# Mamba2 scan and cosine router: two buffers per scan input instead of three, with B's transpose loaded last and two vector steps moved

## The chip, the cores and the metric

The kernel runs on one NeuronCore of a Trainium2 chip. The core has a matrix engine (TensorE, PE in the profile, with its weight loads as PEld), a vector engine (VectorE, DVE), a scalar engine (ScalarE, ACT), a general engine (GpSimd, POOL) and a sequencer that mostly issues DMAs (SyncE, SP). The metric is the device time of one launch in microseconds; lower is better.

## The reference, cut to what matters

The first part is a chunked state-space scan over x (4 batches, 8 heads, 768 steps, 32 wide) with decays `a` and 16-wide matrices B and C. In a chunk, with `cum` the cumulative sum of log(a) and L[i,j] = exp(cum_i − cum_j) for i ≥ j:

```
y_intra = ((C_i · B_j) * L[i,j]) x_j          # inside the chunk
y_inter = exp(cum_i) * (C_i state)            # from the state before the chunk
state   = exp(sum la) * state + sum_j exp(cum_last - cum_j) B_j x_j
```

The second part takes y as 3072 rows of 256. Each row goes to one of 8 experts, by the largest cosine with that expert's embedding, and gets gate * (relu(row w1[e]) w2[e]), where w1 is 256 x 1024, w2 is 1024 x 256 and the gate is the softmax weight of the chosen expert. All data are float32.

## The kernel before, in words

**Scan.** The sequence is cut into six chunks of Q = 128 steps (`NC` = 6), and all batches and heads of a chunk are done together. `load(k, c)` brings in a chunk's five inputs: `ct` (C transposed), `bi` (B transposed), `x`, `xa` (the upper half of x's columns for the chunk's first 64 steps, put on the other half of the partitions) and `b` (B by step). They come from the pool `inp` of three buffers per name, all on SP's queue and in program order. A load into a buffer waits until the readers of the chunk that held it are done. The readers are: `scale_c` on DVE for `ct`; `split_b` on ACT and `inner` on PE for `bi`; `scale_x` and `scale_first_half` on POOL for `x`; `scale_first_half` for `xa`; `sums` on PE for `b`.

`decays` makes cumulative products on DVE for chunks 0 to 3, and later for 4 and 5. `spread_decays` (PE) copies them to all partitions, and `scale_c` multiplies C by them. `inner` (PE) makes the products of C and B into the PSUM tile `pg`, for two batches at a time, and `mask_inner` (DVE, line 341) multiplies them by the causal mask into `g`. `outputs` and `first_outputs` (PE, lines 369 and 382) multiply `g` by the scaled x into `py`; `first_outputs` reads `xb`, a tile of which one half per partition group must be zero. `clear_first_half` zeroes it once for each of its two buffers, and POOL then fills the other half per chunk (line 258). The state lives in `V`: `sums` (PE) makes a chunk's contribution in the PSUM tiles `pz`, `add_sums` (DVE, line 316) adds it to the decayed state `U`, and `decay_states` makes `T` (DVE) and `U` (POOL, line 293) for the next chunk. `finish` (PE, line 400) turns a chunk's outputs to rows and takes their products with the embeddings, half of it in `py` and half in the `pz` banks; `keep_rows` (ACT) and `send_rows` (SP, line 415) bring the rows to memory. `pick`, `count_picks`, `rank_rows`, `places` and `locate` work out each row's expert and its place there.

**Order.** Every engine's instructions run in the order in which the Python program writes them: a manual schedule is in force, and the framework adds waits only. `mamba` is that order. In it, loop step c does chunk c and prepares chunk c + 1; `load(k, c + 2)` stands at the head of the step, and `add_sums(k, c)` stands before the step's first `mask_inner` for c of 3 and 4, and behind `scale_c` of the next chunk for c of 1 and 2. `warm_up` puts matmuls of a constant on PE that nothing reads.

**Experts.** Rows of an expert are gathered by indirect DMA (line 844), turned, multiplied by w1 (line 951) and w2 (lines 968 and 1013; in four of the experts the second product is done in seven block products), turned back and scattered (line 1056). The weights of the first experts are loaded on SP's queue during the scan: w1 of expert 0 at step 3, w2 of expert 0 at step 4.

Of the kernel before, what the change touches and what calls it, by code (L numbers as in the profile page):

```python
# [19 lines left out]
NC = S // Q  # L20
# [19 lines left out]
def load_decays(k):  # L40
    nc = k.nc
    k.a0 = k.mc.tile([128, 2, Q], F32, name="a0")
    a = k.a.rearrange("b h (c s) -> c (b h) s", c=NC)
    nc.gpsimd.memset(k.a0[:, 1, :], 1.0)
    for c in range(NC):
        (nc.sync if c % 2 == 0 else nc.scalar).dma_start(k.a0[c % 4 : 128 : 4, c // 4, :], a[c])


def load(k, c):
    nc = k.nc  # L50
    t = k.ld[c]

    def in_(name, shape):
        return k.inp.tile([128] + shape, F32, name=name, tag=name)

    t.ct, t.bi, t.b = in_("ct", [NB, Q]), in_("bi", [NB, Q]), in_("b", [NB, 128])
    t.x, t.xa = in_("x", [NB, DM]), in_("xa", [NB, 128])
    for dst, src in ((t.ct, k.CT), (t.bi, k.BT), (t.x, k.x)):
        nc.sync.dma_start(dst[:].rearrange("p b m -> p (b m)"), src[c])
    nc.sync.dma_start(t.xa[HQ:, :, :], k.x[c, 0:HQ, :].rearrange("p (b m) -> p b m", b=NB)[:, :, 128:])  # L60
    nc.sync.dma_start(t.b[:].rearrange("p b m -> p (b m)"), k.B[c])


def load_weights(k, e, parts=(0, 1)):
# [60 lines left out]
def clear_first_half(k, i):  # L125
    k.nc.vector.memset(k.xb[i][0:HQ, :, :, 1, :], 0.0)
    k.nc.vector.memset(k.xb[i][HQ:, :, :, 0, :], 0.0)


def warm_up(k, n):  # L130
    for _ in range(n):
        k.nc.tensor.matmul(k.pz[1][:], lhsT=k.warm[:, 0:Q], rhs=k.warm[:], start=True, stop=True)
# [96 lines left out]
def mask_c(k, c):  # L229
    t = k.ld[c]  # L230
    for v in range(2):
        k.nc.scalar.activation(t.cp[:, :, 3 + v, :], t.cp[:, :, 1, :], ACT.Copy, scale=k.tmask[:, v : v + 1])
# [395 lines left out]
def mamba(k):  # L628
    nc = k.nc
    k.f = k.mc.tile([128, 2, FX], F32, name="f")  # L630
    k.rT = k.mc.tile([128, 2, 2, 128], F32, name="rT")
    k.V = k.mc.tile([128, NB, 2 * D], F32, name="V")
    k.ends = k.mc.tile([128, NC, NB, 3], F32, name="ends")
    k.rr, k.wm, k.ends_in = {}, {}, {}
    for c in range(NC):
        k.ld[c] = Net()
        k.ld[c].g = []
    load_decays(k)
    expert_emb(k)
    load(k, 0)  # L640
    build_consts(k)
    warm_up(k, 13)
    decays(k, 0)
    load(k, 1)
    square_emb(k)
    route_consts(k)
    spread_decays(k, 0)
    warm_up(k, 3)
    split_b(k, 0)
    scale_c(k, 0)  # L650
    mask_c(k, 0)
    inverses(k, 0)
    block_ends(k, 0)
    scale_emb(k)
    clear_first_half(k, 0)
    spread_decays(k, 1)
    warm_up(k, 1)
    inner(k, 0, 0)
    mask_inner(k, 0, 0)
    turn_inverses(k, 0, k.py[:, 0, 0:256])  # L660
    scale_x(k, 0, nc.gpsimd)
    scale_first_half(k, 0, nc.gpsimd)
    scale_c(k, 1)
    spread_ends(k, 0, k.pz[0][:, 0:48])
    turn_emb(k, k.pz[1][:, 400:416])
    warm_up(k, 2)

    for c in range(NC):
        t = k.ld[c]
        n = c + 1  # L670
        if c + 2 < NC:
            load(k, c + 2)
        if c in (3, 4):
            load_weights(k, 0, (c - 3,))
        if c == 5:
            load_weights(k, 1, (0,))
        if 2 <= c < NC - 1:
            spread_decays(k, n)
        if 3 <= c < NC - 1:
            add_sums(k, c)  # L680
        if c >= 2:
            inner(k, c, 0)
        if c == NC - 1:
            early_places(k, c - 3)
        if c >= 2:
            mask_inner(k, c, 0)
        if 3 <= c < NC - 1:
            locate(k, c - 3)
            keep_located(k, c - 3)
        if n < NC:  # L690
            scale_x(k, n, nc.gpsimd)
        if 1 <= c < NC - 1:
            scale_c(k, n)
        if c in (1, 2):
            add_sums(k, c)
        if c >= 2:
            pick(k, c - 2)
        if c > 0:
            finish(k, c - 1)
            keep_rows(k, c - 1)  # L700
            send_rows(k, c - 1)
        if c == 2:
            spread_ends(k, 1, k.pz[0][:, 400:424])
        inner(k, c, 1)
        mask_inner(k, c, 1)
        if c == 0:
            sums(k, 0)
        if n < NC:
            split_b(k, n)
            mask_c(k, n)  # L710
        if c == NC - 1:
            k.early_x = early_rows(k)
            gather_halves(k, k.early_x, k.gi0, 0, 0, 3 * NB * Q)
        if c >= 2:
            count_picks(k, c - 2)
        if c == NC - 1:
            gather_halves(k, k.early_x, k.gi0, 0, 1, 3 * NB * Q)
        if n < NC:
            scale_first_half(k, n, nc.gpsimd)
            if c in (0, 3):  # L720
                between(k, n, 4 if c == 0 else NC)
            pass_c(k, n)
        if 3 <= c < NC - 1:
            add_located(k, c - 3)
        if c > 0:
            from_states(k, c)
        if 2 <= c < NC - 1:
            rank_rows(k, c - 2)
            keep_ranks(k, c - 2)
        outputs(k, c, 0)  # L730
        if c == 0:
            clear_first_half(k, 1)
            spread_decays(k, 2)
            inner(k, 1, 0)
            mask_inner(k, 1, 0)
            add_sums(k, 0)
        outputs(k, c, 1)
        if c == NC - 1:
            early = early_jobs(k)
            early[0].turn_x()  # L740
            rank_rows(k, c - 2)
            keep_ranks(k, c - 2)
        first_outputs(k, c)
        keep_outputs(k, c)
        if c + 2 < NC:
            sums(k, n)
        if c == 2:
            turn_inverses(k, 1, k.pz[0][:, 0:256])
        if c == NC - 1:
            pick(k, c - 1)  # L750
            count_picks(k, c - 1)
        if c >= 2:
            places(k, c - 2)
        if c == 4:
            shift_places(k)
        if c == 1:
            decays(k, 1)
            block_ends(k, 1)
            inverses(k, 1)
        if n < NC:  # L760
            decay_states(k, n)
    return early
# [583 lines left out]
@with_exitstack  # L1346
def kernel(
    ctx: ExitStack,
    tc: tile.TileContext,
    x: bass.AP,  # L1350
    a: bass.AP,
    B: bass.AP,
    BT: bass.AP,
    CT: bass.AP,
    moe_expert_emb: bass.AP,
    moe_tau: bass.AP,
    moe_w1: bass.AP,
    moe_w2: bass.AP,
    out: bass.AP,
):  # L1360
    k = Net()
    k.tc, k.nc = tc, tc.nc
    k.x, k.a, k.B, k.BT, k.CT = x, a, B, BT, CT
    k.emb, k.tau, k.w1, k.w2, k.out = moe_expert_emb, moe_tau, moe_w1, moe_w2, out
    k.ld, k.w1t, k.w2t = {}, {}, {}

    k.y_d = tc.dram_tile([T, W], F32, name="y_rows")
    k.of_row = tc.dram_tile([E * T, 1], I32, name="of_row")
    k.const = ctx.enter_context(tc.tile_pool(name="const", bufs=1))
    k.wp = ctx.enter_context(tc.tile_pool(name="wp", bufs=3))  # L1370
    k.ep = ctx.enter_context(tc.tile_pool(name="ep", bufs=1))
    with ExitStack() as m:
        k.mc = m.enter_context(tc.tile_pool(name="mc", bufs=1))
        k.inp = m.enter_context(tc.tile_pool(name="inp", bufs=3))
        k.work = m.enter_context(tc.tile_pool(name="work", bufs=2))
        ps = m.enter_context(tc.tile_pool(name="ps", bufs=1, space=PSUM))
        k.py = ps.tile([128, 2, 512], F32, name="py")
        k.pz = [ps.tile([128, 512], F32, name=f"pz{i}") for i in range(2)]
        k.pgs = m.enter_context(ExitStack())
        k.pg = k.pgs.enter_context(tc.tile_pool(name="pg", bufs=1, space=PSUM)).tile([128, 4, 512], F32, name="pg")  # L1380
        k.late_psum = m.enter_context(ExitStack())
        with tc.manual_schedule():
            early = mamba(k)
            late = scan_end(k, early)
    with (
        tc.tile_pool(name="moe", bufs=2, reuse_waits="tile") as p,
        tc.tile_pool(name="moe_ps", bufs=1, space=PSUM, reuse_waits="tile") as ps,
    ):
        k.p, k.ps = p, ps
        with tc.manual_schedule():  # L1390
            last = moe(k, early[1], late)
        leftover(k)
        with tc.manual_schedule():
            moe_end(k, last)
# [43 lines left out]
```

## Time and profile before

| what | value |
|---|---|
| median of 3 runs | 279.59 us (275.69 to 284.28) |
| the profiled execution's own time | 278.24 us |
| its span, first to last instruction | 276.5 us |
| PE busy | 256.2 us (93%) |
| DVE busy | 148.9 us (54%) |
| POOL busy | 159.0 us (58%) |
| ACT busy | 70.9 us (26%) |
| mean granted PE clock | 0.977 |
| moved by DMA | 35.87 MB, 29.05 MB of it read from HBM |

The scan takes roughly the first 80 us; the rest is the experts. Busy shares are means over both, and a matmul's end in the trace is modelled, so a high PE share does not mean that PE is at its limit. In a row of the timeline the first number is the start and the second the duration, in us; what stands in brackets is the idle time of the engine ahead of it and the engine, tile and line whose end released it. "issue" there means that the trace shows no wait.

### The profile page before, as it was taken

Reading aid. Unit: us, or ns where it says so; the run is one execution under the profiler, and the core shown is the slowest. Engines: PE = TensorE matmul, PEld = TensorE weight load, DVE = VectorE, ACT = ScalarE, POOL = GpSimd, SP = SyncE. Lnnn points to the kernel's source line nnn. Section 1 sums busy time; section 2 is a strip of 40 time slices with the busy share of each in tenths; the row PEclk is TensorE's granted clock in tenths of the full one; section 3 lists DMA queues with packets and bytes.
Section 4 is the critical chain, followed back from the end, with each engine's and each line's share of the span. In section 5 each row is a group of like instructions: output and inputs, shape, how many; then the busy total and the mean of one; then the engine's idle time right before and its main releaser. Section 6 shows DMA issues by size and latency. Waiting matters only on the chain.

```text
span 276.5 us, 6216 instructions
## 1 busy us (share of the span) xinstructions
PE 256.2 (93%) x2446; PEld 209.6 (76%) x2446; DVE 148.9 (54%) x396; ACT 70.9 (26%) x216; POOL 159.0 (58%) x193
## 2 busy tenths in 40 slices
PE   6759989898699999999999999999999999999990
PEld 2548778788599999999469659757957965975890
DVE  5873867888464402144656458468448645833011
ACT  3604344343055132340231131031023123101100
POOL 8998254764503542848828858866956966005022
PEclk9997999999779999999999999999999999999998
DMA  4992849936309920698718518615640201002011
GB/s 120 322 359 59 278 133 274 281 110 163 109 10 282 267 74 9 146 263 189 203 27 183 171 54 177 193 47 124 141 148 26 63 3 53 1 0 56 8 33 31
DMA packets 22304, 35.87 MB, mean 130 GB/s; under 512 B 2548, under 2 KB 15551, under 8 KB 22273
## 3 DMA queue, kind: packets, MB, share of 16 engines
q1 hardware_dynamic: 19024, 28.73, 37.5%
q0 software_dynamic: 3072, 6.67, 9.5%
q8 instruction: 20, 0.33, 0.6%
q14 instruction: 12, 0.09, 0.1%
q10 hardware_dynamic: 176, 0.06, 0.1%
HBM read 29.05 MB, written 6.65 MB: 129 GB/s over the span
## 4 chain that ended last, share of the span: by engine, by line
PE 56%; issue 15%; DVE 10%; POOL 10%; DMA 6%; ACT 1%; POOLq 1%; DVEq 0%
PE hp L951 22%; PE yp L1013 12%; PE eb L951 5%; DMA out_dram<-yo,to 4%; PE eb L968 4%; DVE g L341 3%; POOL xb L258 2%; PE yp L968 2%; DMA xg<-y_rows,gi 2%; POOL xg L844 2%; POOL out_dram L1056 2%; PE py L382 2%; PE pg L331 2%; POOL spread L91 1%; PE ot L1053 1%
## 5 line engine op out<-in xcount | busy, mean ns | idle before, releaser
L951 PE MATMUL hp<-xT,w 128*128 128x416 f32 (+1 forms) x256 | 83.9, 469 | 0.0
L1056 POOL DMA_INDIRECT out_dram<-yo,to x32 | 34.5, 1080 | 55.3 <-DVE yo L1055 54.1
L951 PEld LDWEIGHTS hp<-xT,w 128*128 128x128 f32 x256 | 45.8, 191 | 21.6 <-issue 21.6
L844 POOL DMA_INDIRECT xg<-y_rows,gi x32 | 43.8, 1370 | 15.6 <-issue 7.3
L955 ACT ACTIVATE hT<-hp 128x416 f32<-128x416 f32 (+1 forms) x32 | 15.2, 474 | 81.8 <-PE hp L951 81.7
L957 DVE TENSOR_SCALAR hT<-hp 128x416 f32<-128x416 f32 (+1 forms) x32 | 17.2, 537 | 29.6 <-PE hp L951 29.6
L341 DVE TENSOR_TENSOR g<-pg,mask 128x1536 f32<-128x1536 f32 x12 | 21.1, 1756 | 9.5 <-PE pg L331 9.5
L968 PE MATMUL yp<-hT,w 128*128 128x208 f32 x128 | 23.4, 340 | 0.3 <-PEq L1270 0.3
L968 PEld LDWEIGHTS yp<-hT,w 128*128 128x128 f32 x128 | 22.3, 190 | 0.9 <-issue 0.9
L1013 PE MATMUL yp<-T,S 128*128 128x208 f32 x120 | 22.7, 339 | 0.0
L1013 PEld LDWEIGHTS yp<-T,S 128*128 128x128 f32 x120 | 21.2, 190 | 0.0
L1083 POOL TENSOR_TENSOR gr<-gr,half 104x4 f32<-104x4 f32 x8 | 8.7, 1090 | 14.2 <-ACT sq L1077 14.1
L1013 PE MATMUL yp<-hT,w 128*128 128x208 f32 x80 | 16.1, 344 | 0.2 <-ACT p L1029 0.2
L1013 PEld LDWEIGHTS yp<-hT,w 128*128 128x128 f32 x80 | 13.7, 190 | 1.0 <-ACT p L1029 0.9
L951 PE MATMUL eb<-xT,w 128*128 128x208 f32 x64 | 14.3, 374 | 0.0
L523 POOL TENSOR_TENSOR pre<-pre,ob 128x8 bf16<-128x8 bf16 x24 | 4.8, 199 | 16.3 <-DVE ob L518 14.8
L1077 ACT ACTIVATE sq<-xg 104x256 f32<-104x256 f32 x32 | 13.0, 407 | 0.0
L988 POOL TENSOR_TENSOR S<-w 128x512 f32<-128x512 f32 x10 | 12.7, 1269 | 0.1
L951 PEld LDWEIGHTS eb<-xT,w 128*128 128x128 f32 x64 | 12.0, 207 | 0.2
L968 PE MATMUL eb<-hT,w 128*128 128x208 f32 x64 | 12.0, 341 | 0.0
L246 POOL TENSOR_TENSOR xs<-x,rT 128x1024 f32<-128x1024 f32 x6 | 11.8, 1966 | 0.1
L393 ACT COPY yT<-py 128x512 f32<-128x512 f32 x12 | 6.4, 589 | 20.1 <-PE py L382 20.1
(224 smaller groups left out, 429.3 us busy)
## 6 DMA issues: line engine op xcount, KB each, us to landing
w<-in_moe_w_dram SPq DMA_DIRECT2D x16, 512.0 KB, 6.9
w<-in_moe_w_dram SPq DMA_DIRECT2D x8, 1024.0 KB, 7.6
y_rows<-rows SPq DMA_DIRECT2D x6, 528.0 KB, 4.2
x<-in_x_dram SPq DMA_DIRECT2D x6, 512.0 KB, 6.0
ct<-in_CT_dram SPq DMA_DIRECT2D x6, 256.0 KB, 5.2
bi<-in_BT_dram SPq DMA_DIRECT2D x6, 256.0 KB, 5.1
b<-in_B_dram SPq DMA_DIRECT2D x6, 256.0 KB, 6.2
xa<-in_x_dram SPq DMA_DIRECT2D x6, 128.0 KB, 7.4
```

Of the source, the lines that this page charges most:

```text
L246: engine.tensor_tensor(out=t.xs[:].rearrange("p b (h d) -> p b h d", h=NH), in0=t.x[:].rearrange("p b (h d) -> p b h d", h=NH), in1=r_of(k ...
L341: k.nc.vector.tensor_tensor(out=g[:], in0=k.pg[:, :, 0:384].rearrange("p q (u m) -> p q u m", u=2), in1=k.mask[:].unsqueeze(1).unsqueeze(1 ...
L844: k.nc.gpsimd.indirect_dma_start(out=x, out_offset=None, in_=k.y_d[0:rows, :], in_offset=bass.IndirectOffsetOnAxis(ap=at, axis=0), bounds_ ...
L951: nc.tensor.matmul(t, lhsT=s.w1[:, j, 128 * f : 128 * f + 128], rhs=s.xT[:, j, :], start=(j == 0), stop=(j == KD - 1))
L955: nc.scalar.activation(s.hT[:, f, :], t, ACT.Relu)
L957: nc.vector.tensor_scalar_max(s.hT[:, f, :], t, 0.0)
L968: nc.tensor.matmul(t, lhsT=s.w2[:, f, 128 * j : 128 * j + 128], rhs=s.hT[:, f, r], start=(f == 0), stop=(f == KF - 1))
L988: k.nc.gpsimd.tensor_tensor(out=s.S[:, n], in0=x, in1=y, op=op)
L1013: nc.tensor.matmul(t, lhsT=a[:, f], rhs=b[:, f], start=start and f == 0, stop=(f == 3), skip_group_check=True)
L1056: d = nc.gpsimd.indirect_dma_start(out=k.out[:, :], out_offset=bass.IndirectOffsetOnAxis(ap=s.to[:, i : i + 1], axis=0), in_=y[:], in_offs ...
L1077: s.k.nc.scalar.activation(sq[:], s.x[:, i, :].rearrange("p (j w) -> p j w", j=KD)[:, :, 0:128], ACT.Square, accum_out=s.r[:, i : i + 1],)
L1083: s.k.nc.gpsimd.tensor_tensor(out=s.r[:], in0=s.r[:], in1=s.k.half[0 : s.tr, 0 : s.nt], op=ALU.pow)
```

## The change

Five edits in the scan:

1. The pool `inp` has two buffers per name instead of three.
2. In `load`, `bi` is second for chunks 0 and 1, as before, and last for chunks 2 to 5.
3. `clear_first_half(k, 0)` moves on DVE from behind `scale_emb` to ahead of `decays(k, 0)`.
4. `add_sums(k, 2)` moves on DVE ahead of step 2's first `mask_inner`.
5. The first run of warm-up matmuls is one shorter (12), the last one longer (3).

The order of every other instruction on every engine is the same, the experts included.

```diff
-    for dst, src in ((t.ct, k.CT), (t.bi, k.BT), (t.x, k.x)):
+    def whole(dst, src):
         nc.sync.dma_start(dst[:].rearrange("p b m -> p (b m)"), src[c])
+
+    whole(t.ct, k.CT)
+    if c < 2:
+        whole(t.bi, k.BT)
+    whole(t.x, k.x)
     nc.sync.dma_start(t.xa[HQ:, :, :], k.x[c, 0:HQ, :].rearrange("p (b m) -> p b m", b=NB)[:, :, 128:])
-    nc.sync.dma_start(t.b[:].rearrange("p b m -> p (b m)"), k.B[c])
+    whole(t.b, k.B)
+    if c >= 2:
+        whole(t.bi, k.BT)
...
-    warm_up(k, 13)
+    warm_up(k, 12)
+    clear_first_half(k, 0)
     decays(k, 0)
...
     scale_emb(k)
-    clear_first_half(k, 0)
     spread_decays(k, 1)
...
-    warm_up(k, 2)
+    warm_up(k, 3)
...
-        if 3 <= c < NC - 1:
+        if 2 <= c < NC - 1:
             add_sums(k, c)
...
-        if c in (1, 2):
+        if c == 1:
             add_sums(k, c)
...
-        k.inp = m.enter_context(tc.tile_pool(name="inp", bufs=3))
+        k.inp = m.enter_context(tc.tile_pool(name="inp", bufs=2))
```

## The prediction

> **What bounds the kernel now.** I read the page's slices first, then PE's waits, then the timeline around the longest wait, then the DMA view of that stretch. Of the page, PE's busy share, its granted clock and the DMA share, over 40 slices of 6.9 us:
>
> ```profile
> PE   6759989898699999999999999999999999999990
> PEclk9997999999779999999999999999999999999998
> DMA  4992849936309920698718518615640201002011
> ```
>
> From slice 11 on (76 us) PE is full, so what the edits save before that point comes off the end, unless it is lost on the way. The scan is not full. PE's waits, with total, count and longest in us:
>
> ```profile
> PE py L369 <- issue: 2.5, 1, 2.5
> ...
> PE pz L400 <- DVE V L316: 1.6, 1, 1.6
> ```
>
> The timelines of PE, POOL and DVE show where these two sit and what runs beside them:
>
> ```profile
> 17.57 0.31 PE L369 MATMUL py<-g,xs 128*32 128x64 f32 x6
> 20.38 0.63 PE L369 MATMUL py<-g,xs 128*32 128x64 f32 x26 [2.50 <-issue]
> 20.95 1.44 PE L382 MATMUL py<-g,xb 128*64 128x64 f32 x32
> ...
> 35.70 0.50 PE L400 MATMUL pz<-turn,yT 128*128 128x136 f32 x2 [1.55 <-DVE V L316]
> ```
> ```profile
> 21.93 0.62 POOL L293 TENSOR_TENSOR U<-T,ends 128x256 f32<-128x256 f32 x1 [0.36 <-DVE T L287]
> ```
> ```profile
> 27.56 1.76 DVE L341 TENSOR_TENSOR g<-pg,mask 128x1536 f32<-128x1536 f32 x1 [3.80 <-PE pg L331]
> ...
> 38.68 1.76 DVE L341 TENSOR_TENSOR g<-pg,mask 128x1536 f32<-128x1536 f32 x1 [1.85 <-PE pg L331]
> ```
>
> PE stops in the middle of one group (6 of its 32 matmuls done) with all inputs there. The DMA view of 17.7 to 18.9 us:
>
> ```profile
> q1 hardware_dynamic: 239, 0.43, 99.8%
> q8 instruction: 1, 0.02, 5.5%
> ```
>
> One 16 KB packet of instructions moves just then, through engines that q1 (the input loads) fills. From 13.6 to 17.7 us q1 takes 106.2% and no instruction packet appears. The last row ahead of the stop is the 449th of PE's rows, its semaphore instructions counted; PE's next stop on "issue" (51.41 to 52.04 us) comes exactly 1,536 rows later, 6 x 256. So these are stops for code, at multiples of one block. The block of the first stop would have been asked for at its predecessor's entry, 256 rows earlier, at 13.6 us, while the loads of four chunks (5.6 MB, issued from 2.96 to 16.96 us) kept the DMA at 324 to 343 GB/s until 21 us.
>
> **The change part by part.**
>
> *Two buffers.* Chunks 2 and 3 no longer load at once. SP holds `x` of chunk 2 until POOL has read chunk 0's: `scale_first_half`'s first row ends at 14.60 us (before, SP issued that load at 10.23). Then follow `xa` behind 15.75, `b` (sums of chunk 0 on PE, 14.94) and `bi`, till about 17.4; `ct` of chunk 3 at about 17.5, its `x` behind 18.81. So at 13.6 us two chunks and one `ct` are in flight, 3.0 MB since 3 us, nearly drained at 0.33 MB/us. The code packet then takes about 1 us to start, 1.05 to move and, as at the stall (18.84 to 20.38), 1.5 to be usable: 17.2 us, where PE needs it at 17.7.
>
> [...]
>
> What is late next is POOL. It works without a gap from 7.67 to 21.0 us, which puts `U` of chunk 1 at 21.93 to 22.55 whatever PE does. `V` follows at 22.6 to 23.1 (0.48 us, as chunk 2's). PE without the stop does `outputs` until 18.3, `first_outputs` (1.15 us where the clock is full, at 29.96) until 19.4; ACT's `yT` takes 1.07, the `py` half of `finish` 1.19, until 21.7. Its `pz` half waits for `V`, 23.1 to 24.3, against 26.39 before. So `inner` and the `g` row at 27.56 come 2.1 us sooner. A rest of the stop up to 1.4 us would be hidden (21.7 to 23.1). Nothing can make it more than 2.1. From below I take 1.3, for the clock, as follows.
>
> The window 18.21 to 21.63 held 1.25 us of PE, and in the next one the granted clock is 0.50. [...] Other windows: 1.81 of 3.41 fell, 2.23 held. After the change the window 21.63 to 25.04 holds about 2.0, between these. [...] I take full speed and keep 0.8 for the range.
>
> *B turned last.* `bi(c+2)` waits for `split_b` and step c's second `inner`. Queued behind it on SP are `send_rows(c-1)`, the next chunk's loads and the weights of expert 0. The order is worth something only against `bi` second, where `x` would wait behind it. Slack of each load (landing takes 4.8 to 8.2 us for `x`): `x(2)` issued 14.7, needed 22.51; `x(3)` 18.9 against 31; `x(4)` 26 against 41; `x(5)` 37 against 52; `bi(4)` 35.4 against 44.4. Rows are read by the first gather at 66 us. Cost 0; had `x(2)` landed 3 us late, POOL's idle 5.14 us before chunk 2's `U` takes it.
>
> The weights are the exception. w1 of expert 0 (42.20 us) and w2 (48.19) stood 6 us apart. Now w1 waits behind `bi(5)`, about 45, so `bi`, w1, rows and w2 make one burst of 2.8 MB, 8 us. PE enters a block near 48.8 (52.04 less 3.3); as at the first stop, 4.15 us to start, 1.05 to move, 1.5 to be usable, 55.5 us, needed at 55.1. I charge 0.3; ends: -0.4 (today's 0.41 us stop goes, if it counted) and 2.5.
>
> *States of chunk 2 ahead of the mask.* Now: mask 33.09 to 34.85, `scale_c`, then `V` at 35.36, so `pz` in `finish` waits 1.55 and `inner` starts at 37.44. After: `V` follows `U` at once, then mask (0.5 later), `scale_c` and `pick` (1.08), which ends when it did. PE runs `pz` without waiting, and `inner` is no longer late: `g` at 38.68 comes 1.2 sooner. Chunk 3, already in this order, agrees: `V` 44.12 to second mask 48.49 is 4.37 us; here it would be 33.17 to 37.5. Range 0.8 to 1.3. From then on DVE carries each step (10.7 us from `T` at 42.98 to 53.67), and the shift goes through to the gather.
>
> *Clearing and warm-ups.* The two memsets take 9.63 to 10.74, 1.11 us, and go into DVE's 1.19 us wait for `a` ahead of 3.94: free, at most 0.1. The first mask can start at 9.9 instead of 10.78. One more warm-up (0.29) then ends near 12.45, when `scale_c` is done, so second `inner` comes 0.7 sooner. POOL's gapless row swallows it: 0, at best 0.7. The shorter first run still spans its warm-up (eight slow, four fast matmuls).
>
> Sum: 2.1 + 1.2 + 0 - 0.3 = 3.0 us. The profiled execution took 278.24, so 275.2 on its terms. With it the four times of this kernel are 275.69, 278.24, 279.59, 284.28, middle 278.9: 275.9.
>
> **Rivals.**
>
> *The typical run gains more (30%).* The four times spread by 8.6 us. Waiting for code hangs on what else the DMA does, and a low clock follows each stop; if that makes the spread, a kernel with little of it lands near its fastest: 275.69 - 3.0 = 272.7. For: code and clock are the only waits here that chance moves. Against: the clock also falls at 72.83 to 79.65, behind the gather, which the change leaves.
>
> *No difference (15%).* The stop is not the loads' doing, or the clock falls in its place: 1.2 - 0.3 remains, 278.0. Against: packets at 26.82 and 38.40, with the DMA freer, came with no stop.
>
> *Slower (10%).* Loads that follow their readers come in bursts at the step's end, where PE changes blocks. A full stop costs 2.5 plus some 1.7 for a window of 3.4 us at half clock. Two on the path: 8.4 - 3.3 = 5.1 slower, 284.0. It decides where fetching takes longer than PE needs for a block, 3.6 us at the shortest (38.10 to 41.71). Against: bursts are issued just behind a block's entry, not ahead.
>
> **Numbers.** The forecast has 45%, 273 to 279 on its own. 2%, some 5.6 us, is about what a measurement of this kernel can tell. Under 273.5 lie most of the first rival and a quarter of the forecast: faster 0.40. Slower by 2%: three quarters of the last rival and a little scatter, 0.10. Same 0.50. Range 271 to 281.5: without the fast end of the first rival and most of the last.
>
> **What would show it.** No "issue" row before 20 us in `outputs`; DMA below full at 13.6 us; clock full in 21 to 25; the chunk 1 `g` near 25.5, chunk 2's second near 35.4; `pz` never waiting for `V` in chunk 2; the gather near 63. I am wrong if "issue" waits reappear at 48 to 58, if POOL waits for `x`, or if `U` of chunk 1 moves.

## The result and the profile after

Over 20 runs of each kernel the median went from 279.38 to 276.2 us: a ratio of 0.9876, with a 95% interval of 0.9838 to 0.9914. It is a gain of 1.2%, inside the 2% that the prediction called no change that can be told. The means over all runs went from 279.6 to 276.0 us, 3.6 less with an interval of 1.8 to 5.4. Ratios here compare each kernel's runs within 1.5% of its fastest, which can be nine of ten runs of a kernel that scatters little and 15 of 32 of one that scatters much, so means over all runs stand beside them where the two differ. The profiled execution took 275.46 us where before's took 278.24; its span is 273.7 us (276.5 before), its mean granted PE clock 0.987 (0.977 before). All lines of the code stand 7 further down: `outputs` is now L376, `first_outputs` L389, `mask` L348, `finish` L407, `inner` L338.

The page of the kernel after: PE's busy share, granted clock and DMA share in 40 slices of 6.8 us.

```profile
PE   7987998879799999999999999999999999999990
...
PEclk9999999999799999999999999999999999999997
DMA  3986865894339910889627519526531101002011
```

The two low clock slices at 69 to 83 us have become one, and slice 3 (20 to 27 us) shows a full clock instead of 7. The DMA row is as full as before until 62 us: the same bytes move, later. PE's waits of the kernel after, in total us, count and longest:

```profile
PE pz L407 <- DVE V L323: 1.4, 1, 1.4
...
PE py L389 <- issue: 1.1, 1, 1.1
...
PE pg L338 <- issue: 0.7, 1, 0.7
```

The wait of 2.5 us in `outputs` is gone. The `pz` wait is another one than before's: it is in step 1 now. Two smaller "issue" waits are new. Where they sit, in PE's timeline:

```profile
17.21 0.88 PE L376 MATMUL py<-g,xs 128*32 128x64 f32 x32
18.03 1.15 PE L389 MATMUL py<-g,xb 128*64 128x64 f32 x32
...
20.35 1.19 PE L407 MATMUL py<-turn,yT 128*128 128x136 f32 x8 [0.29 <-ACT yT L400]
22.96 1.19 PE L407 MATMUL pz<-turn,yT 128*128 128x136 f32 x8 [1.42 <-DVE V L323]
```
```profile
56.62 0.33 PE L338 MATMUL pg<-cp,bt 32*128 32x64 f32 x4 [0.71 <-issue]
...
61.53 0.74 PE L389 MATMUL py<-g,xb 128*64 128x64 f32 x18 [1.06 <-issue]
```

`outputs` runs through its 32 matmuls. PE reaches the `pz` half of `finish` at 21.5 and waits for `V` 1.42 us. The timelines of POOL and DVE show why, and what became of the masks:

```profile
21.97 0.62 POOL L300 TENSOR_TENSOR U<-T,ends 128x256 f32<-128x256 f32 x1 [0.36 <-DVE T L294]
```
```profile
25.33 1.76 DVE L348 TENSOR_TENSOR g<-pg,mask 128x1536 f32<-128x1536 f32 x1 [2.22 <-PE pg L338]
...
35.20 1.76 DVE L348 TENSOR_TENSOR g<-pg,mask 128x1536 f32<-128x1536 f32 x1 [0.30 <-PE pg L338]
...
57.40 1.76 DVE L348 TENSOR_TENSOR g<-pg,mask 128x1536 f32<-128x1536 f32 x1 [1.64 <-PE pg L338]
```

`U` of chunk 1 has not moved (21.93 before). The second mask of chunk 1 starts at 25.33 instead of 27.56, the second of chunk 2 at 35.20 instead of 38.68. The lead of 3.48 us then shrinks. It is 2.77 at `U` of chunk 3 (43.47 to 40.70), 1.79 at the mask of 57.40 (59.19 before), and 0.98 at the first gather, on POOL before and after:

```profile
66.17 1.30 POOL L844 DMA_INDIRECT xg<-y_rows,gi  x1 [3.42 <-DVE gi L830]
```
```profile
65.19 1.30 POOL L851 DMA_INDIRECT xg<-y_rows,gi  x1 [5.25 <-DVE gi L837]
```

At the end of the first expert's gathering and turning it is 2.8 again (the last `eb` matmul at 97.06 against 99.86), and from there to the end the two profiles take the same time within 0.05 us. The last part comes from the clock. The table by windows gives the length in us, the busy time of PE, PEld, DVE, ACT and POOL, then PEclk, DMA share and GB/s; first of the kernel before, then of the kernel after:

```profile
72.83:76.24 3.41, 2.92 (x38) 2.74 (x39) 1.27 (x7) 0.67 (x3) 0.94 (x5) 0.50 0.14 35
76.24:79.65 3.41, 3.41 (x13) 3.15 (x14) 2.09 (x10) 1.66 (x5) 0.00 (x0) 0.50 0.02 5
```
```profile
21.05:24.46 3.41, 1.99 (x25) 1.66 (x27) 1.91 (x4) 1.24 (x3) 3.05 (x3) 1.00 0.73 223
...
72.25:75.66 3.41, 3.41 (x40) 3.23 (x38) 2.15 (x9) 1.67 (x4) 0.59 (x3) 0.50 0.16 37
```

Behind the gather the clock was 0.50 for 3.41 us, where before it was 0.50 for 6.83 us. `first_outputs` ran its 32 matmuls in 1.98 us in these stretches (at 74.08 before, 72.40 after) and in 1.15 at full clock (29.96 before, 18.03 after). By my estimate a PE that is busy throughout loses half of 3.41 us to a clock of 0.50, 1.7 us of the difference; the lead grew by 1.8.

### The profile page after: what moved, and what is told of

Same layout as the page of the kernel before. It is cut to its first block, busy times and chain, and to the rows that moved or that the text cites. A ratio compares the mean times of both kernels' runs of the same rounds, so it can differ in the third digit from the quotient of the medians.

```text
span 273.7 us, 6221 instructions
## 1 busy us (share of the span) xinstructions
PE 255.0 (93%) x2446; PEld 207.6 (76%) x2446; DVE 148.7 (54%) x396; ACT 70.9 (26%) x216; POOL 159.0 (58%) x193
## 3 DMA queue, kind: packets, MB, share of 16 engines
q1 hardware_dynamic: 19024, 28.73, 38.4%
## 4 chain that ended last, share of the span: by engine, by line
PE 51%; POOL 16%; issue 16%; DVE 8%; DMA 6%; POOLq 1%; ACT 0%; DVEq 0%
PE hp L958 22%; PE yp L1020 13%; POOL xb L265 5%; PE eb L958 5%; DMA out_dram<-yo,to 4%; PE eb L975 4%; PE yp L975 2%; DMA xg<-y_rows,gi 2%; DVE g L348 2%; POOL xg L851 2%; POOL out_dram L1063 2%; POOL xs L253 1%; POOL spread L98 1%; PE ot L1060 1%; POOL cp L244 1%
## 5 line engine op out<-in xcount | busy, mean ns | idle before, releaser
L964 DVE TENSOR_SCALAR hT<-hp 128x416 f32<-128x416 f32 (+1 forms) x32 | 17.2, 537 | 29.6 <-PE hp L958 29.6
L348 DVE TENSOR_TENSOR g<-pg,mask 128x1536 f32<-128x1536 f32 x12 | 21.1, 1755 | 7.1 <-PE pg L338 7.1
L958 PE MATMUL eb<-xT,w 128*128 128x208 f32 x64 | 13.4, 357 | 0.0
L958 PEld LDWEIGHTS eb<-xT,w 128*128 128x128 f32 x64 | 11.4, 199 | 0.1
L975 PEld LDWEIGHTS eb<-hT,w 128*128 128x128 f32 x64 | 11.1, 191 | 0.0
```

Source lines behind the costliest of these rows:

```text
L348: k.nc.vector.tensor_tensor(out=g[:], in0=k.pg[:, :, 0:384].rearrange("p q (u m) -> p q u m", u=2), in1=k.mask[:].unsqueeze(1).unsqueeze(1 ...
L958: nc.tensor.matmul(t, lhsT=s.w1[:, j, 128 * f : 128 * f + 128], rhs=s.xT[:, j, :], start=(j == 0), stop=(j == KD - 1))
L964: nc.vector.tensor_scalar_max(s.hT[:, f, :], t, 0.0)
L975: nc.tensor.matmul(t, lhsT=s.w2[:, f, 128 * j : 128 * j + 128], rhs=s.hT[:, f, r], start=(f == 0), stop=(f == KF - 1))
```

## The experiments

The theory: PE stops at the edge of a block of 256 of its rows while that block's packet waits behind loads; with the stop gone, POOL's `U` is what is late; the early states take another 1.2 us; what is lost later are code stops of the same kind at other blocks. (Block n is the one whose edge lies behind PE's row 256 n - 63: the stop of the kernel before is at block 2, row 449, its small one at 52.04 us at block 8, row 1,985. No trace shows the request for a packet. "Asked for" stands for PE's passing of the edge ahead: up to the first gather each of the two profiles has ten packets of 16 KB for the ten blocks from block 2 on, and they start from 0.06 us ahead of that passing (26.82 against 26.88) to 4.16 us behind it (17.78 against 13.62) in the kernel before, and from 0.16 ahead (24.49 against 24.65) to 5.49 behind (54.12 against 48.63) in the kernel after.) The rivals: the stop belongs to the work done there and not to code; the loads don't cause it; one edit alone makes the gain; B turned last has a part in it.

### Loads that nobody reads

Five more loads of 512 KB, into tiles that nothing reads, behind those of chunk 1 in the kernel after. The computation is unchanged.

```diff
+    unread = [k.mc.tile([128, NB * DM], F32, name=f"unread{i}") for i in range(3)]
+    for i in range(5):
+        nc.sync.dma_start(unread[i % 3][:], k.x[i])
```

> The kernel after with five loads of 512 KB that nothing reads, on SP's queue where chunk 2's loads stood before; everything else as after. Theory (code waits behind load traffic): the code packet asked for at 13.3 us starts at 16.5 or later (after 15.07), PE stops 1.5 to 3 us in outputs at the same row as before, and chunk 1's second mask starts at 26.3 to 28. Rival (the stop went because loads wait for their readers or their order changed, not for their amount): stop under 0.5 us, mask at 25.3 to 25.7.

One run took 284.31 us. PE's timeline of this kernel:

```profile
16.77 0.31 PE L376 MATMUL py<-g,xs 128*32 128x64 f32 x6
18.99 0.63 PE L376 MATMUL py<-g,xs 128*32 128x64 f32 x26 [1.91 <-issue]
```

The stop is back, 6 of 32 matmuls into `outputs`, behind the same 449th row as before. PE entered the preceding block at 12.83 us; the packet of code moved from 16.59 to 17.62, and DMA was full meanwhile (the input queue at 105.1% from 12.8 to 16.6 us). The second mask of chunk 1 came at 27.07. So bytes in the queue make the stop, with nothing about the buffers' number changed. The run also had stops at blocks 4, 9 and 10 (2.1, 1.0 and 3.0 us of wait), and POOL waited 3.9 us for `x` of chunk 2, which stood behind the unread loads. So what this one run took above the 275.46 of the kernel after, 8.9 us, is not the price of the first stop.

### Six more warm-up matmuls ahead of the stop

In the kernel before, the last run of warm-ups is 8 long instead of 2: 12 more PE rows ahead of the stop.

```diff
-    warm_up(k, 2)
+    warm_up(k, 8)
```

> The kernel before with six more warm-up matmuls (12 more rows on PE, nothing reads them) in the last run of warm-ups. [...] Rival (outputs waits for data that the trace does not name): it stops after 6 matmuls of outputs as before, behind row 461.

```profile
17.39 0.46 PE L331 MATMUL pg<-cp,bi 32*128 32x128 f32 x8
20.00 0.65 PE L369 MATMUL py<-g,xs 128*32 128x64 f32 x32 [2.15 <-issue]
```

The stop stayed behind the same count of PE rows, 449, as I had expected, and so moved in the work: from behind the 6th matmul of `outputs` to ahead of its first. I had placed it further up, in `inner`; six matmuls are 12 rows, and 12 rows back is just the head of `outputs`. The stop at block 8 also kept its row count (1.6 us of wait) and so came 12 rows earlier in the work. So it is the position in the instruction stream that stops PE, not the operation that happens to stand there.

### Two buffers alone, twice

The kernel before with `bufs=2` and the new order of loads that goes with it (its lines are those of the change).

```diff
-        k.inp = m.enter_context(tc.tile_pool(name="inp", bufs=3))
+        k.inp = m.enter_context(tc.tile_pool(name="inp", bufs=2))
```

> The kernel before with the two buffers and B transposed last, nothing else. Theory (the loads of chunks 2 and 3 held up PE's code): the stop of 2.5 us in outputs is gone or under 0.5; the second mask of chunk 1 starts at 25.2 to 25.7 us (before 27.56, after 25.33); the pz half of finish in step 2 still waits for V, so the second mask of chunk 2 starts near 36.6 (before 38.68, after 35.20); PE stops for code again between 54 and 62, as after. Ratio to before 0.990 to 0.996. Rival (the clearing, the warm-ups or the state step move the chunk 1 mask): the stop stays, the mask stays at 27.5, ratio 1.00.

> The kernel two_buffers_only once more, for its time. Theory (0.9991 in the first comparison came from scatter and from late code stops): the stop in outputs is absent and chunk 1's second mask stands at 25.2 to 25.9 again; ratio to before 0.988 to 0.998. Rival (the saving is given back for good at blocks 9 and 10): these two stops together over 3 us again, the first gather no sooner than 66 us, ratio 0.998 to 1.005.

Ratios of 0.9991 (0.9918 to 1.0064) and 1.0052 (1.0010 to 1.0093): no gain in time, short of what was expected both times; over all runs of both, 278.9 us against 278.9 before. There is no stop at the second block, and in both profiles the second mask of chunk 1 is at 25.33, as in the kernel after. That of chunk 2, expected near 36.6, came at 36.45 in the second profile, and at 37.47 in the first, where PE ran at half clock from 35.05. The first profile, PE in step 2 and at block 10:

```profile
30.72 1.19 PE L407 MATMUL py<-turn,yT 128*128 128x136 f32 x8
33.47 0.73 PE L407 MATMUL pz<-turn,yT 128*128 128x136 f32 x4 [1.55 <-DVE V L323]
...
62.91 0.68 PE L389 MATMUL py<-g,xb 128*64 128x64 f32 x14
66.85 1.23 PE L389 MATMUL py<-g,xb 128*64 128x64 f32 x18 [3.26 <-issue]
```

The wait for `V` in step 2 is still there with its old 1.55 us. So the states' edit has something of its own to take. At block 10 PE stops for 3.26 us: the packet was asked for at 59.73 and started at 63.92. Then the clock is at 0.5 for 10.24 us from 65.77, and the first gather, at 72.59, is 6.4 us later than in the kernel before. In the second profile blocks 9 and 10 came without a stop and the gather at 65.06. One kernel, two executions, 7.5 us apart at the gather.

### States of chunk 2 alone, twice

The kernel before with only `add_sums(k, 2)` moved.

```diff
-        if 3 <= c < NC - 1:
+        if 2 <= c < NC - 1:
             add_sums(k, c)
...
-        if c in (1, 2):
+        if c == 1:
             add_sums(k, c)
```

> The kernel before with chunk 2's state step ahead of its first mask, nothing else. Theory: the stop of 2.5 us in outputs stays, chunk 1's second mask stays at 27.4 to 27.7; pz in step 2 no longer waits for V, chunk 2's second mask starts 1.1 to 1.4 us sooner, at 37.3 to 37.6. Ratio 0.993 to 0.999. Rival (the step is carried by DVE's own work): that mask moves under 0.5 us.

> The kernel states_only once more, for its time. Theory (1.0057 came from code stops that chance made long, 0.99 and 3.42 us at blocks 6 and 7): the stop in outputs stays, pz of step 2 does not wait for V, chunk 2's second mask comes 9.6 to 10.0 us behind chunk 1's (before 11.12); ratio 0.993 to 1.001. Rival (the edit itself makes those stops long): over 3 us of stops at blocks 6 and 7 again, ratio over 1.003.

Ratios of 1.0057 (1.0006 to 1.0109) and 1.0083 (1.0032 to 1.0134): slightly slower (over all runs of both, by 1.6 us, with an interval of 0.0 to 3.1). Locally the edit did what it should. The second mask of chunk 2 follows that of chunk 1 after 9.62 and 9.63 us, where it took 11.12 in the kernel before; that is 1.5 us. (The marks themselves scattered: 38.13 and 36.43, with 37.3 to 37.6 expected.) Then the first profile:

```profile
48.32 0.33 PE L331 MATMUL pg<-cp,bt 32*128 32x64 f32 x3
51.80 0.48 PE L331 MATMUL pg<-cp,bt 32*128 32x64 f32 x3 [3.15 <-issue]
```

A stop at block 7 (asked for at 42.21, packet from 49.06) takes back more than was gained. It was there in the second profile too, 2.6 us (asked 40.51, packet from 46.67), and block 8 brought another 2.12. So the rival that I set against chance, that the edit itself makes these stops, held. With three buffers, and with w1 and w2 of expert 0 loading at their old places, the earlier PE meets the edge of block 7 in the middle of a burst. From 42.2 to 49.1 us of the first profile the input queue took 95.9%. In no other profile of this study does block 7 stop PE. Both profiles are of executions slower than this kernel's median (282.08 and 282.45 us against 280.38 and 279.46), so they may show more of the loss than is typical.

### Buffers and states without the clearing

The kernel after, with the clearing and the warm-ups put back.

```diff
-    warm_up(k, 12)
-    clear_first_half(k, 0)
+    warm_up(k, 13)
...
+    clear_first_half(k, 0)
...
-    warm_up(k, 3)
+    warm_up(k, 2)
```

> The kernel after with the clearing and the warm-ups where they stood before, so two buffers and the state step alone. Theory (the clearing is worth nothing behind POOL's gapless row): chunk 1's second mask at 25.2 to 25.7, chunk 2's second mask at 35.0 to 35.9, as after (25.33, 35.20); code stops at blocks 9 and 10 (55 to 62 us) of 1 to 4 us together; ratio to before 0.984 to 0.994. Rival (the clearing carries the gain, since neither other part had one alone): ratio 0.997 or more.

The ratio is 0.9878 (0.9809 to 0.9948), that of the whole change. DVE's timeline of this kernel has both landmarks within half a microsecond of the whole change:

```profile
25.81 1.76 DVE L348 TENSOR_TENSOR g<-pg,mask 128x1536 f32<-128x1536 f32 x1 [2.22 <-PE pg L338]
...
35.67 1.76 DVE L348 TENSOR_TENSOR g<-pg,mask 128x1536 f32<-128x1536 f32 x1 [0.30 <-PE pg L338]
```

No stop of 0.2 us or more on "issue" is left up to the gather, which is issued at 64.97; I had expected 1 to 4 us of them at blocks 9 and 10. The two edits together reach the gain of the whole change, though neither alone has any.

### Clearing and warm-ups alone

```diff
-    warm_up(k, 13)
+    warm_up(k, 12)
+    clear_first_half(k, 0)
...
-    clear_first_half(k, 0)
...
-    warm_up(k, 2)
+    warm_up(k, 3)
```

> The kernel before with the clearing ahead of the decays and the warm-ups moved, nothing else. Theory: first mask 0.3 to 0.9 us sooner than 10.78, U of chunk 1 within 0.1 us of 21.93, chunk 1's second mask within 0.7 us of 27.56, the stop in outputs still there; ratio 0.995 to 1.005. Rival (it carries the gain): ratio under 0.993.

The ratio is 0.9949 (0.9887 to 1.0011), which tells nothing from no change. But over all its ten runs the mean is 276.6 us against 279.3, 2.7 less with an interval of 0.7 to 4.7, and close to the 276.0 of the kernel after. Its mean clock, 0.981, is as high as that kernel's; set to one clock, as in the table further down, it gains nothing (276.7 against 276.8). So the times alone do not refute the rival here. What speaks against it is the kernel above, which has the gain without the clearing. The landmark missed what I expected, 27.56 within 0.7: it came 1.15 sooner, at 26.41. PE's timeline shows how:

```profile
16.99 0.31 PE L369 MATMUL py<-g,xs 128*32 128x64 f32 x6
19.22 0.63 PE L369 MATMUL py<-g,xs 128*32 128x64 f32 x26 [1.92 <-issue]
```

PE enters the block ahead of the edge at 13.06 instead of 13.62, the packet starts at 16.33 instead of 17.78, and the stop ends 1.16 us earlier. `U` of chunk 1 stays at 21.92. I had said that POOL swallows what the clearing gains. That holds where POOL is what comes last; with three buffers the stop comes last, and there the clearing is worth something.

### B turned second

The kernel after with `bi` second in every chunk.

```diff
-    if c < 2:
-        whole(t.bi, k.BT)
+    whole(t.bi, k.BT)
...
-    if c >= 2:
-        whole(t.bi, k.BT)
```

> The kernel after with B transposed loaded second for all chunks, as before, and two buffers. Theory (the order matters by what stands behind B transposed on SP's queue): x of chunk 3 is issued near 25.8 instead of 18.88 us, x of chunk 4 near 35.7, x of chunk 5 near 46, each landing within 1 us of POOL's need of it (31, 41, 52), so POOL waits for x by up to 1.5 us in a step, and PE asks for code while x, xa and b move: masks of chunks 3 and 4 come 0 to 2 us later than after; ratio to before 0.988 to 0.998. Rival (the order is worth nothing): every mask within 0.3 us of after's up to chunk 3, ratio 0.984 to 0.991.

The ratio is 1.0063 (1.0027 to 1.0099) to the kernel before; the mean over all runs is 277.5 us, between before's 279.0 and after's 276.0. SP's queue of this kernel (DMA issues):

```profile
26.97 0.33 SPq L59 DMA_DIRECT2D bi<-in_BT_dram  x1
27.39 0.38 SPq L59 DMA_DIRECT2D x<-in_x_dram  x1
```

`x` of chunk 3 now stands behind `bi` and is issued at 27.39, not 18.88; the next two come at 37.02 and 47.54. POOL waits for the first of them, once and briefly:

```profile
32.94 1.97 POOL L250 TENSOR_TENSOR xs<-x,rT 128x1024 f32<-128x1024 f32 x1 [0.45 <-DMA x<-in_x_dram]
```

In the kernel after POOL never waits for `x`. The wait of 0.45 us cost nothing further on: the second masks of chunks 1 and 2 are at 26.95 and 36.57, late by 1.62 and 1.37, and the first of these comes ahead of that wait and behind a low clock at 23.30. The stop at block 10 is 1.75 us and the gather is issued at 67.03.

Is the place of `bi` worth time, then? The ratios, 0.9876 for the whole change and 1.0063 here, have intervals that don't meet. But the means over all runs differ by 1.5 us with an interval of 0.1 to 3.0, in sessions of their own, and set to one clock by 0.3 us (276.2 and 276.5 in the table further down). This leans to a small loss and does not show one; that it would go through code stops and the clock is argued from one profile.

### The weights at their old distance, and POOL's next

First, the kernel after with w1 of expert 0 ahead of the loads of chunk 5, w2 at step 4 and expert 1's w1 in the scan's end, away from block 10. Second, the same with `route_consts` moved off the head of POOL's stream to step 1, behind the first pass.

```diff
+        if c == 3:
+            load_weights(k, 0, (0,))
...
-        if c in (3, 4):
-            load_weights(k, 0, (c - 3,))
-        if c == 5:
-            load_weights(k, 1, (0,))
+        if c == 4:
+            load_weights(k, 0, (1,))
...
-    load_weights(k, 1, (1,))
+    load_weights(k, 1)
+    second.w1 = k.w1t[1]
```
```diff
-    route_consts(k)
...
+        if c == 1:
+            route_consts(k)
```

> The kernel after with expert 0's w1 loaded ahead of chunk 5's inputs instead of behind them, and expert 1's w1 behind the last rows of the scan instead of at 56 us. Theory (bunched weights hold up PE's code after the change): the stops at blocks 9 and 10 (0.92 and 1.28 us after) are under 0.4 each, the first gather is issued at 62.5 to 63.8 us (after 65.19), no wait of PE for expert 1's weights near 90; ratio to before 0.974 to 0.985. Rival (those stops are beside DVE's chain and cost nothing): gather at 65, ratio as after, 0.988.

> The kernel weights_spread with POOL's route constants (2.9 us of small instructions ahead of chunk 0's scaling) moved behind chunk 2's pass_c in step 1, into POOL's idle time. Theory (POOL's gapless row swallows what the clearing frees): chunk 0's scaling starts at 10.6 to 10.9 us instead of 11.62, U of chunk 1 at 21.0 to 21.3 instead of 21.97, chunk 1's second mask near 24.5, everything behind it 0.7 to 1.0 us sooner; ratio to before 0.970 to 0.982. Rival (DVE or PE bounds there as well): U of chunk 1 moves under 0.3 us or the mask of chunk 1 does not follow.

> The kernel both once more, for its time (0.982 with an interval of 0.966 to 0.998). Theory: U of chunk 1 at 21.1 to 21.4, first gather at 62.5 to 64 us; ratio to before 0.972 to 0.984. Rival (no better than after): 0.985 or more.

Weights alone: 0.9898 (0.9833 to 0.9962). Both: 0.9820 (0.9662 to 0.9978) and 0.9906 (0.9871 to 0.9941), with medians of 271.91 against 279.87 and 273.49 against 278.19. Moving the weights took the stops at blocks 9 and 10 away and put one at block 8, in PE's timeline of the first:

```profile
48.94 0.74 PE L389 MATMUL py<-g,xb 128*64 128x64 f32 x17
50.98 0.68 PE L389 MATMUL py<-g,xb 128*64 128x64 f32 x15 [1.30 <-issue]
```

The gather of this profile is issued at 64.38, not at the 62.5 to 63.8 that I expected, and the ratio missed its range as well. With the weights moved, none of three profiles stops at block 9 or 10, and each of them stops at block 8 (1.30, 1.35 and 2.15 us). That fits the weights as the cause of the two stops but is not the whole of it: buffers and states, and the second profile of two buffers, pass both edges with the weights bunched, behind a window at half clock (from 53.54 and from 54.58) that brought PE there later. Later, the expert's weights were not waited for. With `route_consts` moved, POOL starts chunk 0's scaling at 10.77 instead of 11.62, and DVE's second mask of chunk 1 hardly moves:

```profile
25.23 1.76 DVE L348 TENSOR_TENSOR g<-pg,mask 128x1536 f32<-128x1536 f32 x1 [2.87 <-PE pg L338]
```

I expected that mask near 24.5. `U` came 0.75 us sooner (21.22), but 0.6 us of the stop at the second block was back, and a window at half clock from 18.25. In the second execution there was no such window and the mask came at 24.79; its gather, expected by 64, came at 68.04, behind the stop of 2.15 us and 10.24 us at half clock. Its ratio, 0.9906, fell to the rival, no better than after. By its medians this is the fastest kernel tried; its intervals overlap those of the change itself.

## Why the prediction was right, and which term was not

**The stop and what is late next: right.** The packet of the second block started about 15.1 and its first row ran at 17.46, with 17.2 predicted. The rest of the stop is at most 0.15 us. `U` stayed (21.97), the slack of 1.4 us was there to a hundredth (1.42 of waiting for `V`), and the mask came 2.23 us sooner, with 2.1 predicted. One premise was off: the loads were not nearly drained when the packet was asked for. From 13.27 to 15.07 us the input queue still took 88.0% (106.2% in the kernel before), and the fetch waited 1.8 us, not 1. The slack covered that. The unread loads brought 1.91 us of wait back by load traffic alone.

**The clock: right by luck.** I took the windows of the kernel before for those of the kernel after. The stretches between two changes of the clock last 3.41 us or multiples of it (17.07, 3.41, 47.79, 6.83 and 194.56 us in the profile before; 64.85, 3.41 and 194.56 after), but their edges lie elsewhere in each execution (21.63 us before; counted back from 72.25, 21.05 after). The window that mattered, 21.05 to 24.46, held 1.99 us of PE, about the 2.0 that I had put, and the clock stayed full. No run shows the 0.8 us that the range keeps for a fall there; the profile after has 1.00 from 7.40 to 72.25 us. My two rows gave a limit between 1.81 and 2.23 us. The other profiles show none: half clock came behind windows with 1.97 us (both, from 14.84), 2.20 (two buffers, second, from 51.17) and 2.46 (buffers and states, from 9.17), and full clock behind 1.85 (buffers and states, from 70.61) and 1.91 (two buffers, second, from 68.23). What decides it stays open.

**States of chunk 2: right.** 1.2 predicted; 1.5 us between two masks, in two profiles of the edit alone, and 1.25 (3.48 less 2.23) in the kernel after.

**B turned last: right that no load is waited for.** The other half of that term, that the order is worth something against `bi` second, is small where it can be seen (one wait of 0.45 us for `x`) and not settled in time.

**Clearing: right in the sum, by a reason that holds only beside two buffers.** With three, the stop comes last and not POOL. The shorter first run of warm-ups was not eight slow matmuls and four fast ones: in the profile after their weight loads stood 0.43 us apart to the last, at 5.74, and the clock was full from 7.40, where before it was full from 4.56 and the last five loads took 1.01 us. `U` of chunk 1 stayed in its place even so.

**The weights: this term was mis-sized.** I charged 0.3 us for one stop (my own figures, 55.5 less 55.1, make 0.4), with an end of 2.5. The profile after has two, and "issue" waits at 48 to 58 us were the first sign that I had named of being wrong. The DMA view of the 5.5 us from 48.63, when PE entered the block ahead, and of the 1.1 us after that:

```profile
q1 hardware_dynamic: 600, 1.27, 87.0%
```
```profile
q1 hardware_dynamic: 373, 0.37, 102.7%
q8 instruction: 1, 0.02, 6.2%
```

No instruction packet moves in the first stretch. The fetch waited 5.5 us behind w1, rows and w2, where I took the 4.15 of the first stop; PE stood 0.71 us at the edge. At block 10, which the prediction left out, w1 of expert 1 was issued at 56.06, half a microsecond ahead of the block's request at 56.61, and PE stood 1.06. Together 1.8 us instead of 0.3. This refutes what I had held against the slower rival, that bursts are issued just behind a block's entry: here both were issued ahead of it (w1, rows and w2 at 46.13 to 48.20, the entry at 48.63). The expectation for the gather, 63, failed by this: it came at 65.19. Another 0.7 us of the lead went on DVE at 37 to 39 us, where operations of `places` took longer than before (L569 0.87 us against 0.17, L575 0.45 against 0.16, and L564 0.22 against 0.51).

**What made up for it was the clock behind the gather,** which I had left where it was: 3.41 us at half speed instead of 6.83, worth 1.8. So the sum of 3.0 us met 2.8 on the profiles, by 1.0 from the scan and 1.8 from a stretch that I had charged at nothing. The mechanisms of the first 36 us were right, and that the total fits as well is luck: behind the gather the same work ran at half clock for two windows in the kernel before, for one in the kernel after and with the clearing alone, and for none in the profiles of six more warm-ups, of two buffers' second run, of buffers and states and of the weights moved.

**Runs scatter by the clock.** The first rival said that chance in code and clock makes the spread. Its words that a low clock follows each stop fit one of the two stops of its profile: half clock came from 21.63 us, behind the stop of 2.50, and the clock was 1.00 from 25.04 to 72.83, behind the one of 0.41. Each run lists its mean granted clock. Over the runs of each kernel a fit of time on clock gives 242 us per unit, give or take 11. One window of 3.41 us at half clock lowers the mean by 0.5 x 3.41 / 276 = 0.0062, so it goes with 1.5 us. Fitted so, the scatter of the kernel before falls from 3.2 to 1.8 us. The table has all runs that list a clock; the last column sets them to 0.98, and is uncertain by 0.2 to 0.5. The stops are PE's "issue" waits of 0.2 us and more from 16 us to the first gather, in the profile or the two.

| kernel | runs | mean us | mean clock | stops, us | us at clock 0.98 |
|---|---|---|---|---|---|
| before | 77 | 279.0 | 0.971 | 2.9 | 276.8 |
| two buffers | 10, 12 | 279.9, 278.1 | 0.965, 0.970 | 4.1, 0 | 276.3, 275.8 |
| states | 10, 12 | 280.4, 280.4 | 0.973, 0.970 | 5.7, 6.8 | 278.7, 278.1 |
| clearing | 10 | 276.6 | 0.981 | 2.3 | 276.7 |
| buffers and states | 10 | 274.9 | 0.976 | 0 | 273.9 |
| after | 20 | 276.0 | 0.981 | 2.0 | 276.2 |
| B second | 10 | 277.5 | 0.976 | 1.8 | 276.5 |
| weights spread | 10 | 274.8 | 0.983 | 1.3 | 275.6 |
| both | 4, 8 | 273.3, 273.9 | 0.987, 0.988 | 1.9, 2.2 | 275.0, 275.8 |

Between before and after, 0.010 of clock goes with 2.4 of the 3.0 us in the means, much as 1.8 of 2.8 did in the two profiles. At one clock the kernel with the most stops (states) is the slowest, and buffers and states, without any in its profile, the fastest. This is an association: no run here held the clock fixed, and a stop delays PE and empties a window at once. Part of the higher clock may be the change's own doing: of the six profiles with a stop of over 1 us in `outputs`, five have a stretch at half clock that begins between 20.0 and 21.7 us; of the eight without it, three have one that begins between 18 and 25. The rival's cause of the spread agrees with all this. It was wrong that this kernel has little of it: its mean clock is 0.981, and its median lies 4.35 us above its fastest run of 271.85.

**What stays open.** Why two edits that give 0.988 together give nothing or a small loss alone is only argued: each alone shifts PE against the traffic so that later edges fall into bursts, as its profiles show. No run takes all later stops away from a single edit. Open too are the worth of `bi`'s place, and how much of the higher clock, which goes with most of the gain in the means, the change brings about and how much is chance.

## What to carry to other kernels

Here a fetch of code moved as a transfer among the others: in the kernel before a packet of 16 KB waited 4.16 us where loads took 106.2% of the DMA engines (13.6 to 17.7 us), and 0.3 us where they had just taken 14.7% (37.5 to 38.4). So find the edges by counting rows on the engine, note when PE passes the edge ahead of each, and look at what the DMA holds just then, for every edge up to the end of the stage and not only for the one that stops today. A microsecond saved early moved all later edges against the loads here, so follow the lead from landmark to landmark before trusting a sum. A part tested alone can show the right landmark and no time; judge its mechanism by the landmark and its worth beside the other parts.

## What the runs showed of the hardware that was not expected

- The stop for code was tied to the row count: 12 more rows ahead of it moved it 12 rows up in the work, behind the same row, the 449th (six more warm-ups, 2.15 us). Unread loads brought 1.91 us of it back at the same row.
- One 16 KB packet waited from 0.3 us (the kernel before, 58.40 to 58.69) to 6.85 us (states, first profile, 42.21 to 49.06) for its start and took 0.93 to 1.60 us to move in the profiles before and after. There the first row of a stopped PE ran 1.17 to 1.54 us after its end.
- PE's busy time in a window of 3.41 us did not tell the clock of the next one: half clock followed windows with 1.25 (the kernel before, from 18.21) to 2.46 us of PE (buffers and states, from 9.17), full clock followed some with 1.85 (buffers and states, from 70.61), 1.91 (two buffers, second, from 68.23) and 1.99 (after, from 21.05). Windows half busy and more were followed by half clock: 1.75 us in the kernel after (from 68.84), 1.81 before (from 69.42).
- A low stretch lasted 3.41 us (the kernel before, from 21.63), 6.83 (before, from 72.83) or 10.24 (two buffers, first profile, from 65.77), one, two or three windows. By the fit above each window goes with about 1.5 us of the whole time, an estimate.
